# A transformer block on one Trainium2 core: four attention pieces moved by one or two steps among the matmuls of the feed-forward part

## The chip, the cores and the metric

The kernel runs on one core of a Trainium2 chip. The core has five engines with instruction queues of their own: TensorE (PE in the profile; its weight loads are PEld), VectorE (DVE), ScalarE (ACT), GpSimd (POOL) and SyncE (SP). Each engine works through its queue in order and waits for the others only by semaphores. The metric is device time in microseconds for one execution, and lower is better.

## What is computed

Eight batches of attention over 576 positions with 8 heads of 64 columns; heads 0 to 3 look at the last 32 positions (the "plain" heads), heads 4 to 7 at every fourth of the last 128 positions (the "dilated" heads). The result, as 4608 rows of 512, goes through two matrices of 512 x 2048 and 2048 x 512 with x·sigmoid(x) between them. Inputs and output are float32.

```python
def _attn_ref(q, k, v):                      # (8, 8, 576, 64)
    scores = scale * np.matmul(q, k.transpose(0, 1, 3, 2))
    rel = pos[:, None] - pos[None, :]
    mask_plain = (rel >= 0) & (rel < window)                                  # window 32
    mask_dil = (rel >= 0) & (rel < window * dilation) & (rel % dilation == 0) # dilation 4
    masks = np.stack([mask_plain if h < H // 2 else mask_dil for h in range(H)], axis=0)
    scores = np.where(masks[None, :, :, :], scores, -1000000000.0)
    scores = scores - np.max(scores, axis=-1, keepdims=True)
    attn = np.exp(scores)
    attn = attn / (np.sum(attn, axis=-1, keepdims=True) + 1e-09)
    return np.matmul(attn, v).astype(np.float32)

def _moe_ref(x, w_in, w_out):                # x: (4608, 512)
    h = x @ w_in
    g = h * (1.0 / (1.0 + np.exp(-h)))
    return (g @ w_out).astype(np.float32)
```

## The kernel before

The kernel goes through the batches 0 to 7. For each it runs layer 1 of the feed-forward part (`layer1`, 16 slices `f` of 128 hidden columns, each of 8 matmuls and one Silu on ScalarE into `gT`) and layer 2 (`layer2`, one row tile `t` of 128 rows after the other, 16 matmuls each, then `store`: a copy from PSUM to `ob` on VectorE and a DMA out on SyncE's queue). Batch 0 is cut in two halves in layer 1 (`layer1_part`), and its layer 2 (`layer2_first`) goes round its first four tiles in groups of four matmuls, in the order of tiles 0, 2, 1, 3. Odd batches take five tiles (4 to 8), since two batches share nine tiles of rows; even batches take four.

The attention of later batches is written in between, by hand. Every batch `b` has a table, `plan_of(b)`, that says at which step which function is issued: `at(step, function, arguments)`. `plan(s)` issues what the table holds for step `s`, in the order in which `at` was called. A step of layer 1 is one slice `f` (steps 0 to 15, 8 matmuls of 128x288); a step of layer 2 is four matmuls of 128x512 (steps 16 on, four to a row tile). In batch 0 the steps from -16 to 15 are the two halves of layer 1, and 16 to 31 the groups of layer 2. What a step issues comes ahead of that step's own matmuls. No planner reorders anything: the order of the calls is the order in each engine's queue (`tc.manual_schedule()`); semaphores only add the waits for data and for buffers.

For a batch `b` and a half `z` of the heads (`z` 0 plain, `z` 1 dilated) the functions are, in their order:

- `load_qk`, `load_v`, `shift_v`: DMAs on POOL's queue (batch 1's `shift_v` on SP's) into `n` (queries and keys as they lie in memory) and `vw` (values).
- `transpose(b, z, which, copies)`: 36 or so TensorE transposes of `n` (L274) for keys and as many for queries, and two copies each from PSUM to `kT`/`qT` (L278) or `kC`/`qC` (L287), by the engines in `copies`.
- `scores(b, z)`: 72 or 80 small matmuls (L324 plain, L336 dilated) into PSUM `s` and `ss`; then on VectorE scale and mask into `ms` (L448, L457) and the negated maxima `nm` (L464).
- `shift(b, z, hi)` (batch 1's dilated half alone) and `exps(b, z, hi)`: the exponentials on ScalarE, with their sums `l`; one instruction for each of 8 or 10 slots (L496), or one in all where `shift` went before (L487).
- `normal(b, z, hi)`: on VectorE the reciprocal `r` of the sums (L509, L510; with L505 a sum ahead of it where `shift` was used) and the weights `pn` (L512).
- `turn(b, z, hi)`: 4 or 5 TensorE transposes of `pn` (L521); `turned`: a copy of them from PSUM into `ptT` (L529).
- `values(b, z)`: 64 small matmuls (L554) and 8 or 16 more (L618) into PSUM `x` and `xs`; `finish`: casts of these into `xT` (L631, L623, L625), which layer 1 of that batch reads.

PSUM has two pools: `big` (two buffers of two banks) for the two layers' results, and `ps` (four buffers of one bank) for everything of the attention. The buffers of a pool are handed out in turn, in the order of the calls.

`plan_of(0)` holds the rest of batch 0's attention and all of batch 1's; `plan_of(1)` all of batch 2's, and of batch 3 the plain transposes, scores and exponentials; `plan_of(2)` to `plan_of(6)` the rest of batch `b + 1` and the beginning of batch `b + 2`. `later` writes the steps of `normal`, `turn`, `turned`, `values` and `finish`: its four numbers are the steps of the two `normal`, of both turns, and of the values. Without other `copies`, `later` gives the `turned` copies and the casts to VectorE.

Of the kernel before, what the change touches and what calls it, by code (L numbers as in the profile page):

```python
# [28 lines left out]
def kernel(  # L29
# [690 lines left out]
    dve, act = both = (nc.vector.tensor_copy, nc.scalar.copy)  # L720

    def transposes(at, b, z, step):
        for which in (1, 0):
            at(step, transpose, b, z, which, both)

    def later(at, b, z, steps, copies=(nc.vector.tensor_copy, nc.vector.tensor_copy)):

        for hi in (0, 1):
            at(steps[hi], normal, b, z, hi)
        for hi in (0, 1):  # L730
            at(steps[2], turn, b, z, hi)
        for hi in (0, 1):
            at(steps[2], turned, b, z, hi, copies[hi])
        at(steps[3], values, b, z)
        at(steps[3], finish, b, z, copies)

    def plan_of(b):
        ev = {}

        def at(s, fn, *args):  # L740
            ev.setdefault(s, []).append((fn, args))

        def all_exps(b, z):
            for hi in (0, 1):
                at(16, exps, b, z, hi)

        if b == 0:

            at(-16, normal, 0, 1, 1)
            at(-15, shift_class, 0, dve, 1, 2)  # L750
            at(-14, normal, 0, 0, 1)
            at(-13, clear_v, 1, nc.vector)
            at(-13, load_v, 1)
            for c in (2, 3):
                at(-13, load_w_out, c)
            at(-13, load_qk, 2)
            at(-8, turn, 0, 1, 1)
            at(-8, turned, 0, 1, 1, act)
            at(-6, values0, 1, 1)
            at(-6, last_values, 0, 1, (1,))  # L760
            at(-6, finish0, 1, 1)
            at(-6, last_finish, 0, 1, 1)
            at(-4, turn, 0, 0, 1)
            at(-4, turned, 0, 0, 1)
            at(-2, values0, 0, 1)
            at(-2, last_values, 0, 0, (1,))
            at(-2, finish0, 0, 1, both)
            at(-2, last_finish, 0, 0, 1)
            transposes(at, 1, 1, 2)
            at(8, scores, 1, 1)  # L770
            for hi in (0, 1):
                at(8, shift, 1, 1, hi)
            for which in (1, 0):
                at(16, transpose, 1, 0, which, (dve, dve))
            at(19, scores, 1, 0)
            at(14, shift_v, 1, nc.sync.dma_start)
            at(15, load_qk, 3)
            at(15, load_v, 2)
            at(15, shift_v, 2, nc.gpsimd.dma_start)
            all_exps(1, 1)  # L780
            for hi in (0, 1):
                at(19, exps, 1, 0, hi)
            for n, z, hi in ((20, 1, 0), (20, 1, 1), (26, 0, 0), (28, 0, 1)):
                at(n, normal, 1, z, hi)
            for n, z, copies in ((27, 1, (dve, dve)), (30, 0, both)):
                for hi in (0, 1):
                    at(n, turn, 1, z, hi)
                for hi in (0, 1):
                    at(n, turned, 1, z, hi, both[hi])
                at(n + 1, values, 1, z)  # L790
                at(n + 1, finish, 1, z, copies)
        elif b == 1:
            transposes(at, 2, 0, 2)
            transposes(at, 2, 1, 10)
            transposes(at, 3, 0, 15)
            at(7, scores, 2, 0)
            at(17, load_qk, 4)
            at(17, load_v, 3)
            at(17, shift_v, 3, nc.gpsimd.dma_start)
            at(13, scores, 2, 1)  # L800
            all_exps(2, 0)
            all_exps(2, 1)
            at(23, scores, 3, 0)
            at(23, exps, 3, 0, 0)
            at(23, exps, 3, 0, 1)
            later(at, 2, 0, (22, 24, 27, 28))
            later(at, 2, 1, (29, 31, 33, 34))
        else:
            if b + 2 < B:
                at(16, load_v, b + 2)  # L810
                at(16, shift_v, b + 2, nc.gpsimd.dma_start)
            if b + 1 < B:
                if b == 2:
                    for n in (0, 1):
                        at(1 + 2 * n, transpose, 3, 1, 1 - n, both)
                later(at, b + 1, 0, (0, 0, 4, 6))
                if b + 3 < B:
                    at(16, load_qk, b + 3)
            if b + 2 < B:
                transposes(at, b + 2, 0, 14)  # L820
                at(17, scores, b + 2, 0)
                at(18, exps, b + 2, 0, 0)
                at(18, exps, b + 2, 0, 1)
            if b + 1 < B:
                at(11, scores, b + 1, 1)
                all_exps(b + 1, 1)
                later(at, b + 1, 1, (22, 24, 27, 28))
            if b + 2 < B:
                transposes(at, b + 2, 1, 30)

        def plan(s):
            for fn, args in ev.pop(s, ()):
                fn(*args)

        return plan
# [58 lines left out]
    for b in range(B):  # L894
        plan = plan_of(b)
        if b == 0:
            for x in range(NFF):
                plan(2 * x - NFF)
                plan(2 * x + 1 - NFF)
                layer1_part(2 * x % NFF, 2 * x // NFF, None if x else warm)  # L900
        else:
            for f in range(NFF):
                plan(f)
                layer1(b, f)
        if b == 0:
            layer2_first(plan)
        else:
            layer2(b, plan)
        for s in range(NFF, 3 * NFF):
            plan(s)  # L910
# [30 lines left out]
```

## Time and profile before

| | us |
|---|---|
| median of three runs | 325.57 (325.37 to 326.73) |
| the profiled execution | 326.71 |
| its span, first to last instruction | 324.9 |
| TensorE busy in it (matmuls) | 309.6 |
| ScalarE, VectorE, POOL busy | 214.9, 179.8, 83.3 |

The stages of the span and how busy the engines were in each, from the windows of the trace:

| us from the start | what runs on TensorE | PE busy | DVE busy | ACT busy | DMA share |
|---|---|---|---|---|---|
| 12 to 41 | batch 0's attention and layer 1 | 26.9 of 29.0 | 21.0 | 20.3 | 1.34 |
| 41 to 61 | layer 2 of batch 0, batch 1's attention | 18.9 of 20.0 | 17.3 | 11.7 | 1.20 |
| 61 to 103.4 | batch 1's layers, attention of 2 and 3 | 41.3 of 42.4 | 25.9 | 36.1 | 0.69 |
| 103.4 to 141 | batch 2's layers, attention of 3 and 4 | 36.9 of 37.6 | 22.6 | 28.7 | 0.62 |
| 254.6 to 288 | batch 6's layers, attention of 7 | 33.1 of 33.4 | 15.4 | 19.7 | 0.09 |
| 288 to 325 | batch 7's layers | 33.2 of 37.0 | 4.2 | 10.7 | 0.12 |

The DMA share is the mean number of packets in work on each of the 16 DMA engines; over 1 means that packets overlap. A group of matmuls ends, by the trace's model, some 0.1 to 0.2 us after the next group has begun, so starts are compared with starts. The span and the profiled execution's time differ by what lies before the first and behind the last instruction (1.8 us).

### The profile page before, as it was taken

To read this page: it belongs to the slowest core of one execution; us is meant where nothing else is said; L and a number is where in the kernel's file an instruction comes from. 1 tells how busy PE (TensorE), PEld (TensorE's weight loads), DVE (VectorE), ACT (ScalarE), POOL (GpSimd) and SP (SyncE) were. 2 spreads that over 40 slices of the span, in tenths; PEclk is the share of its full clock that TensorE was granted. 3 is DMA by queue.
4 is the path that set the end of the run, shared out by engine and by line. 5 is a ranking of instruction groups with operands and counts; after the bars stand their busy time and mean duration, and the time that the engine had idled before them with its cause. 6 is when DMAs were issued, how large, how long until landed. Compare 5 with 4: busy or idle time off the path is not lost.

```text
span 324.9 us, 11768 instructions
## 1 busy us (share of the span) xinstructions
PE 309.6 (95%) x5151; PEld 200.5 (62%) x5151; DVE 179.8 (55%) x379; ACT 214.9 (66%) x700; POOL 83.3 (26%) x140
## 2 busy tenths in 40 slices
PE   5679989999989999999999999999999999999995
PEld 2458745677446774577645776567745776467544
DVE  6896679736497555762675446672577423530011
ACT  2676657666998568975797458985699357726300
POOL 8536537418304430245005600051000000000000
PEclk9679999999999999999999999999999999999999
DMA  8999999928924990298219850191011100110021
GB/s 110 184 214 204 190 230 202 234 70 130 173 86 77 134 146 2 100 148 133 45 65 121 182 88 2 67 170 39 5 39 62 65 4 0 68 67 0 2 97 67
DMA packets 45668, 32.63 MB, mean 100 GB/s; under 512 B 21264, under 2 KB 40336, under 8 KB 45616
## 3 DMA queue, kind: packets, MB, share of 16 engines
q0 software_dynamic: 39520, 21.73, 48.7%
q1 hardware_dynamic: 5952, 10.08, 8.4%
q8 instruction: 40, 0.66, 0.8%
q14 instruction: 12, 0.10, 0.1%
q10 hardware_dynamic: 144, 0.07, 0.1%
HBM read 37.75 MB, written 9.44 MB: 145 GB/s over the span
## 4 chain that ended last, share of the span: by engine, by line
PE 83%; DVE 6%; ACT 5%; DMA 3%; issue 2%; POOL 1%; POOLq 0%
PE h L644 35%; PE o L707 30%; PE h L664 4%; PE t L274 3%; ACT pe L496 3%; PE x L554 3%; DMA n<-in_q_dram 2%; PE pt L521 2%; DVE pn L512 1%; PE s L324 1%; PE o L681 1%; PE s L336 1%; DVE ms L448 1%; DVE nm L464 1%; PE x L580 1%
## 5 line engine op out<-in xcount | busy, mean ns | idle before, releaser
L644 PE MATMUL h<-xT,w_in 128*128 128x288 f16 x896 | 115.6, 286 | 0.7 <-issue 0.7
L707 PE MATMUL o<-w_out,gT 128*128 128x512 f16 (+1 forms) x528 | 115.6, 373 | 0.0
L652 ACT ACTIVATE gT<-h 128x576 f16<-128x576 f32 x112 | 73.0, 651 | 63.7 <-PE h L644 63.0
L644 PEld LDWEIGHTS <-w_in 128*128 128x128 f16 x896 | 85.6, 98 | 23.9 <-issue 1.0
L496 ACT ACTIVATE pe<-ms,nm 128x64 f32<-128x64 f32 x246 | 81.6, 333 | 3.3 <-DVE nm L464 3.2
L707 PEld LDWEIGHTS <-gT 128*128 128x128 f16 x528 | 50.1, 98 | 53.0
L691 DVE COPY ob<-o 128x512 f32<-128x512 f32 (+1 forms) x36 | 24.5, 682 | 53.4 <-PE o L707 53.1
L496 ACT ACTIVATION_READ_ACCUMULATOR pe<-ms,nm 128x1 f32 x246 | 45.9, 187 | 0.0
L448 DVE SCALAR_TENSOR_TENSOR ms<-s,mask 128x512 f32<-128x512 f32 x28 | 19.2, 686 | 44.2 <-PE s L336 26.1
L127 POOL DMA_DIRECT2D vw<-in_v_dram x16 | 10.1, 639 | 79.2 <-PE x L554 78.0
L512 DVE TENSOR_TENSOR pn<-pe,r 128x640 f16<-128x640 f32 (+2 forms) x32 | 25.3, 792 | 1.1
L631 DVE CAST xT<-x 128x512 f16<-128x512 f32 x27 | 17.4, 685 | 11.2 <-PE xs L618 11.2
L464 DVE TENSOR_REDUCE nm<-ms 128x10 f32<-128x640 f32 (+1 forms) x28 | 22.0, 787 | 1.0
L106 POOL DMA_DIRECT2D n<-in_k_dram x28 | 16.6, 607 | 15.5 <-PE t L274 5.9
L106 POOL DMA_DIRECT2D n<-in_q_dram x28 | 16.4, 606 | 10.1 <-DMA w_out<-in_moe_w_out_dram 5.3
L664 PE MATMUL h<-xT,w_in 128*128 128x256 f16 (+1 forms) x128 | 17.1, 286 | 1.3 <-ACT gT L671 1.3
L529 DVE COPY ptT<-pt 128x640 f16<-128x640 f16 (+1 forms) x27 | 11.8, 468 | 8.2 <-PE pt L521 8.0
L664 PEld LDWEIGHTS <-w_in 128*128 128x128 f16 x128 | 12.1, 98 | 5.1 <-issue 2.0
L681 PE MATMUL o<-w_out,gT 128*128 128x512 f16 x64 | 14.8, 380 | 0.1
L671 ACT ACTIVATE gT<-h 128x512 f16<-128x512 f32 (+1 forms) x16 | 10.3, 650 | 6.9 <-PE h L664 6.8
L521 PE MATMUL pt<-ident,pn 128*128 128x128 f16 x152 | 12.4, 224 | 1.4 <-DVE pn L512 1.4
L274 PEld LDWEIGHTS <-n 64*64 64x64 f16 (+1 forms) x840 | 10.0, 101 | 5.5 <-issue 5.1
(102 smaller groups left out, 264.7 us busy)
## 6 DMA issues: line engine op xcount, KB each, us to landing
out_dram<-ob SPq DMA_DIRECT2D x35, 256.0 KB, 2.0
n<-in_k_dram POOLq DMA_DIRECT2D x28, 144.0 KB, 5.5
n<-in_q_dram POOLq DMA_DIRECT2D x28, 144.0 KB, 5.7
vw<-in_v_dram POOLq DMA_DIRECT2D x8, 288.0 KB, 6.5
vw<-in_v_dram POOLq DMA_DIRECT2D x16, 128.0 KB, 4.2
w_in<-in_moe_w_in_dram POOLq DMA_DIRECT2D x4, 512.0 KB, 12.1
w_out<-in_moe_w_out_dram POOLq DMA_DIRECT2D x4, 512.0 KB, 10.6
vw<-vw POOLq DMA_DIRECT2D x12, 128.0 KB, 3.4
```

Source lines behind the costliest of these rows:

```text
L106: nc.gpsimd.dma_start(out=qk[b, z, which][i * HF : i * HF + UPS[z]].rearrange("p h u d -> p h (u d)"), in_=src[b, h : h + 2].rearrange("h ...
L274: nc.tensor.transpose(dst, w, ident[r, r])
L448: nc.vector.scalar_tensor_tensor(out=ms[:, 0:8].rearrange("p (n t) c -> p n (t c)", n=2), in0=s[hi].rearrange("p n t c -> p n (t c)"), sca ...
L464: nc.vector.tensor_reduce(out=nm[:, 0:w], in_=ms[:, 0:w], axis=AX.X, op=ALU.max, negate=True)
L496: nc.scalar.activation(pe[:, t, :], slot(t), AF.Exp, scale=1.0 if b else scale, bias=nm[:, t : t + 1], accum_out=l[:, t : t + 1],)
L512: nc.vector.tensor_tensor(pn[:, 0:w], a["pe", z, hi][:, 0:w], r[:, 0:w, None].broadcast_to([P, w, KB]), ALU.mult)
L521: nc.tensor.transpose(t[:, i, :], a["pn", z, hi][:, 2 * i : 2 * i + 2].rearrange("p t c -> p (t c)"), ident)
L644: nc.tensor.matmul(h[:, half, 0:HS], w_in16[:, c, f * P : f * P + P], xT[:, c, half * HS : half * HS + HS], start=(c == 0), stop=(c == MC ...
L652: nc.scalar.activation(gT[:, f, s0 : s0 + S].rearrange("p (a c) -> p a c", a=2), h[:, :, 0:HS], AF.Silu)
L664: nc.tensor.matmul(h[:, i, 0 : c1 - c0], w_in16[:, c, (f + i) * P : (f + i + 1) * P], xT[:, c, c0:c1], start=(c == 0), stop=(c == MC - 1),)
L691: copy(ob, o)
L707: nc.tensor.matmul(o, gT[:, f, t * P : (t + 1) * P], w_out16[:, f, m0:m1], start=(f == 0), stop=(f == NFF - 1),)
```

## The change

Four pieces of the table get other steps. No function changes, and no instruction is added or taken away.

- Batch 1 (table of batch 0): the plain transposes go from step 16 to 17, the plain scores and exponentials from 19 to 20. The dilated half's values and casts go from 28 to 29 (`n + 1 + z` with `z` 1); the plain half's stay at 31.
- Batch 3 (table of batch 1): plain scores and exponentials from step 23 to 21, ahead of the first `normal` of batch 2's plain half (22).
- Batch 3 (table of batch 2): dilated scores from step 11 to 10.
- Batch 7 (table of batch 6): turn and `turned` of the dilated half from step 27 to 28, values and casts from 28 to 29.

```diff
@@ plan_of, b == 0
             for which in (1, 0):
-                at(16, transpose, 1, 0, which, (dve, dve))
-            at(19, scores, 1, 0)
+                at(17, transpose, 1, 0, which, (dve, dve))
+            at(20, scores, 1, 0)
...
             for hi in (0, 1):
-                at(19, exps, 1, 0, hi)
+                at(20, exps, 1, 0, hi)
...
-                at(n + 1, values, 1, z)
-                at(n + 1, finish, 1, z, copies)
+                at(n + 1 + z, values, 1, z)
+                at(n + 1 + z, finish, 1, z, copies)
@@ plan_of, b == 1
-            at(23, scores, 3, 0)
-            at(23, exps, 3, 0, 0)
-            at(23, exps, 3, 0, 1)
+            at(21, scores, 3, 0)
+            at(21, exps, 3, 0, 0)
+            at(21, exps, 3, 0, 1)
@@ plan_of, b >= 2
-                at(11, scores, b + 1, 1)
+                at(10 if b == 2 else 11, scores, b + 1, 1)
                 all_exps(b + 1, 1)
-                later(at, b + 1, 1, (22, 24, 27, 28))
+                later(at, b + 1, 1, (22, 24, 28, 29) if b == 6 else (22, 24, 27, 28))
```

## The prediction, made before the changed kernel was run

> **What bounds the kernel now.** I read the page first (here its span, its busy times and its instruction queue), then the waits of TensorE alone (who waited for whom, us in total, times, longest), then the timeline around each wait (start, duration, engine, line, operation, in brackets the idle time before it), and last the packet times of the instruction queue.
>
> ```profile
> span 324.9 us, 11768 instructions
> PE 309.6 (95%) x5151; PEld 200.5 (62%) x5151; DVE 179.8 (55%) x379; ACT 214.9 (66%) x700; POOL 83.3 (26%) x140
> ...
> q8 instruction: 40, 0.66, 0.8%
> ```
>
> ```profile
> PE pt L521 <- DVE pn L512: 1.4, 2, 1.1
> PE h L664 <- ACT gT L671: 1.3, 1, 1.3
> PE t L274 <- issue: 0.8, 1, 0.8
> PE h L644 <- issue: 0.7, 1, 0.7
> ```
>
> TensorE is busy 95% of the span, and after the first 40 us it stops at only four places that are worth naming: twice for `pn` (1.11 and 0.33 us), and twice for "issue", which is no engine and no DMA (0.83 us at L274, 0.70 us at L644). A step that moves work is worth what it does to one of these four, or to a wait that it makes.
>
> What is "issue"? 0.66 MB in 40 packets is 16.4 KB each, and 10,302 TensorE instructions over 40 packets are 258 each, so queue 8 brings TensorE's program in blocks of about 256 instructions, 128 pairs of load and matmul. Counted in the trace, the two pauses come at weight loads 739 and 2276, which are 12 x 128 + 1 apart: both are block edges. The block for the first was fetched from 40.26 to 41.15 us and TensorE went on at 42.61; the block for the second from 121.13 to 122.06, and it went on at 123.38. So a block is usable 1.3 to 1.5 us after it landed. In both cases the fetch began late: 4.0 and 4.2 us after the preceding edge, with DMA loads running. With the DMA engines idle it began about 1.0 to 1.4 us after TensorE was 16 pairs short of the edge.
>
> **Part A, batch 1** (plain transposes 16 to 17, plain scores and exps 19 to 20, dilated values and finish 28 to 29). TensorE's timeline there:
>
> ```profile
> 41.23 0.54 PE L274 MATMUL t<-ident,n 64*64 64x64 f16 x44
> 42.61 0.41 PE L274 MATMUL t<-ident,n 64*64 64x64 f16 x28 [0.83 <-issue]
> 42.95 2.76 PE L681 MATMUL o<-w_out,gT 128*128 128x512 f16 x12
> 45.65 0.68 PE L324 MATMUL s<-kT,qT 64*32 64x64 f16 x64
> ...
> 53.26 0.88 PE L521 MATMUL pt<-ident,pn 128*128 128x128 f16 x10
> ```
>
> The pause falls 44 transposes into the 72. One step is four 128x512 matmuls; the 28 ahead of part B's scores (81.22 to 87.35) took 6.13 us, 0.87 a step. After the change these four run ahead of the transposes, so the same edge comes 40 transposes in, at about 41.23 + 0.9 + 0.3 = 42.45. The block is usable at 42.61 as before: the pause shrinks from 0.83 to about 0.1. But the transposes then end at 43.0, as before, twelve matmuls still stand between them and the scores, and the scores start at 45.7 as before. From there VectorE works without a hole from 46.40 to 59.25 (scores, sums, `pn`, `ptT`, casts of `xT`, stores, in its own timeline), and layer 1 of batch 1 starts at 60.88 behind its last casts. That chain starts no sooner, so TensorE only reaches the turn of the dilated part 0.87 earlier, at 52.4, and waits for `pn` (ready 53.62) instead. The values at 29 let `ob` of tile 0 go before the casts on VectorE; the same 3.07 us of work lies between 56.2 and 59.25, in another order. The copies of the transposed `kT`,`qT` (1.42 + 1.41 us) end at 45.5, 0.2 before the scores. The exps follow the scores on ScalarE, and the two `pn` of the dilated part still stand behind the scores' VectorE work. Taken: **0.0**. Bounds: -0.83 (the whole pause kept as gain) to +0.87 (pause not a fetch: it travels, and the chain starts a step later). I take the middle, since both ends need the fetch or the full VectorE to be misread.
>
> **Part B, batch 3's plain scores from 23 to 21 in batch 1's steps.**
>
> ```profile
> 87.35 0.68 PE L324 MATMUL s<-kT,qT 64*32 64x64 f16 x64
> 87.85 0.27 PE L324 MATMUL ss<-kT,qT 64*32 64x64 f16 x8
> 88.05 3.63 PE L707 MATMUL o<-w_out,gT 128*128 128x512 f16 x16
> 91.51 0.39 PE L521 MATMUL pt<-ident,pn 128*128 128x128 f16 x4
> 93.01 0.45 PE L521 MATMUL pt<-ident,pn 128*128 128x128 f16 x5 [1.11 <-DVE pn L512]
> ```
>
> The turn waits for a `pn` that VectorE reaches late, behind 3.06 us of score work (88.11 to 91.17) and an `ob` copy. Two steps earlier the scores start at 85.62 and VectorE at 86.38, 1.73 sooner; but `pn` of the first half (86.17 to 87.30, 1.13 us, until now done before the scores) then stands behind them. In sum: 86.38 + 3.06 + 1.10 + 0.63 (`ob`, overlapped) + 1.19 = 92.3 against 92.95. The wait goes from 1.1 to about 0.5: **-0.6**. The first half's `pn` is ready at 90.5, one microsecond before its turn at 91.51. Inputs of the scores are there since 81.6. ScalarE runs exps without a hole from 83.38 to 101.9 either way. Bounds: -1.1 (wait gone) to 0.
>
> **Part C, batch 3's dilated scores from 11 to 10 in batch 2's steps.** Nothing waits there for scores. But the block edge ahead of load 2276's lies in them (load 2147, at 116.94). With eight 128x288 matmuls fewer ahead of it (0.98 us, less eight more score pairs), this edge comes 0.85 us earlier, and the next fetch can begin at 120.3 instead of 121.13 (the same 4.2 us behind its edge) and be usable at 120.3 + 0.9 + 1.3 = 122.5, while TensorE reaches load 2276 at 122.3 to 122.6. **-0.7.** Bounds: -0.8 to 0.
>
> **Part D, batch 7's turn 27 to 28, values 28 to 29.**
>
> ```profile
> 281.76 0.44 PE L521 MATMUL pt<-ident,pn 128*128 128x128 f16 x5
> 282.53 0.45 PE L521 MATMUL pt<-ident,pn 128*128 128x128 f16 x5 [0.33 <-DVE pn L512]
> 282.82 1.03 PE L707 MATMUL o<-w_out,gT 128*128 128x512 f16 x4
> 283.78 0.71 PE L554 MATMUL x<-ptT,vw 64*64 64x32 f16 x64
> ```
>
> A step later the turn starts at 282.63 and finds `pn` ready (282.47). From its first matmul to the next group's it took 1.06 instead of the 0.56 of batch 2's turn at 99.26: 0.50 is saved. But `ob` of tile 2 now goes ahead of the two `ptT` copies on VectorE (0.69 from about 282.8, then 0.89), which end at 284.4; TensorE is there at 283.19 + 0.96 = 284.15 and waits 0.25, with the last tile's twelve matmuls and all of layer 1 queued behind the values. **-0.25.** Bounds: -0.5 to +0.1. The casts to `xT` end at 286.6, layer 1 of batch 7 starts after 287.
>
> No moved step issues a DMA. POOL's loads that reuse batch 1's `n` start at 49.28, six microseconds after the transposes that read it, and its loads after the values start at 77.75 at the soonest.
>
> **Sum:** 0.0 - 0.6 - 0.7 - 0.25 = -1.55, so the span goes from 324.9 to about 323.4. The profiled execution took 326.71, the median 325.57; the difference is taken from the median: **324.0**. About 0.5% (1.63 us) is what a measurement of this kernel can tell from no change; the limits are 323.9 and 327.2.
>
> **Rivals.**
>
> R1, the pauses aren't fetches. Then the first travels with the transposes (+0.83, VectorE's chain a step later) and the second stays: 0.83 - 0.6 - 0.25 = 0.0, **325.6**. For it: the profile names no cause. Against: both pauses stand 128-pair multiples apart, in the middle of a tile, where no buffer and no load can hold TensorE. [...]
>
> R2, the second fetch starts no sooner, because it waits for the loads to drain: at 121.0 they did drain. For it: the same at 190.27. Against: at 83.78 and 46.34 a fetch began amid loads. C gives 0: **324.7**.
>
> R3, batch 1's VectorE chain has slack that I don't see, and A's 0.83 stays gained: **323.2**. For: TensorE's own waits there are 0.1 to 0.3. Against: no hole on VectorE.
>
> R4, slower. In part A the request for the block after load 739 goes out 0.9 us later, behind more loads. It is needed at load 867, which TensorE now reaches at 49.0, with 0.9 of slack before `pn`. Fetch 1.2 and 1.3 until usable: a start by 47.4 costs nothing (it was 46.34), each microsecond later costs one, and from 48.95 on the kernel is slower. Behind the key load issued at 41.52, which landed at 52.04, it would start at 51: +3.6, **327.6**. Against: the fetch of before went past key loads that landed at 51.32.
>
> **Chances.** Forecast 0.55 (its own range 323.5 to 324.5), R1 0.14, R2 0.15, R3 0.10, R4 0.06. The range 323.0 to 325.6 takes in R1 to R3 and leaves out R4 and the ends of the others. Faster by over 0.5%: 0.30 of the forecast, all of R3, 0.02 of R2, 0.42. Slower: R4 and 0.02 of R1, 0.08. The rest, 0.50, is within.
>
> **What would show it.** A: fewer than 0.2 us of "issue" in L274 near 42.5, scores at 45.7, and a wait of about 0.9 at the dilated turn. B: the wait before the second five transposes about 0.5. C: no "issue" before L644 in batch 2, its block landing before 121.5. D: no wait at batch 7's turn, about 0.25 at its values. Scores of batch 1 at 46.5 would make A's reading wrong; a pause that stays in batch 2, C's.

## The result, and the profile after

The changed kernel took 325.06 us (median of 20 runs, 323.34 to 326.57), the kernel before 326.1 in the 20 runs beside it (325.25 to 328.37): a ratio of 0.9967, with a 95% interval of 0.9953 to 0.9982, which is 0.6 to 1.5 us less. A second comparison, told below, gave 0.9948 (0.9928 to 0.9968). Both intervals leave out 1, so it is faster, but by less than the 0.5% that I had named as the limit of what can be told in the first comparison and by about that much in the second.

The page of the changed kernel, its span and busy times:

```profile
span 322.8 us, 11769 instructions
PE 311.8 (97%) x5151; PEld 202.0 (63%) x5151; DVE 180.1 (56%) x379; ACT 214.7 (67%) x700; POOL 83.2 (26%) x140
```

Its waits of TensorE (who waited for whom, us in total, times, longest), the two rows that can be set beside those of before:

```profile
PE pt L521 <- DVE pn L512: 1.2, 2, 0.7
...
PE h L664 <- ACT gT L671: 0.5, 1, 0.5
```

Both rows with "issue" are gone. There are still two waits for `pn`, but other ones: the 0.7 is new and stands in batch 1, the other 0.44 is what is left of the 1.11. The wait at L664 lies in batch 0, where nothing was moved; it was 1.3 before and is 1.2 in a second trace of the changed kernel, so its 0.8 is no effect of the change. TensorE's timeline of the changed kernel at the four places (start, duration, engine, line, operation, idle time before it):

```profile
41.88 0.93 PE L274 MATMUL t<-ident,n 64*64 64x64 f16 x72
...
45.44 0.68 PE L324 MATMUL s<-kT,qT 64*32 64x64 f16 x64
...
52.30 0.44 PE L521 MATMUL pt<-ident,pn 128*128 128x128 f16 x5
53.48 0.45 PE L521 MATMUL pt<-ident,pn 128*128 128x128 f16 x5 [0.74 <-DVE pn L512]
...
85.40 0.68 PE L324 MATMUL s<-kT,qT 64*32 64x64 f16 x64
...
92.11 0.45 PE L521 MATMUL pt<-ident,pn 128*128 128x128 f16 x5 [0.44 <-DVE pn L512]
...
120.14 2.13 PE L644 MATMUL h<-xT,w_in 128*128 128x288 f16 x16
122.11 1.03 PE L707 MATMUL o<-w_out,gT 128*128 128x512 f16 x4
...
280.73 0.72 PE L521 MATMUL pt<-ident,pn 128*128 128x128 f16 x10
281.29 1.03 PE L707 MATMUL o<-w_out,gT 128*128 128x512 f16 x4
282.24 0.92 PE L554 MATMUL x<-ptT,vw 64*64 64x32 f16 x64
```

All 72 transposes of batch 1 now run in one piece, the plain scores start when they did before, and TensorE waits at the dilated turn instead. Batch 3's plain scores start 4.41 us behind layer 2 of batch 1 (80.99 to 85.40) instead of 6.13. The last 16 matmuls of batch 2's layer 1 have no hole. Batch 7's turn runs in one piece, and its values take 0.92 where they take 0.71 elsewhere.

Spans of single executions differ by a microsecond or more (324.0 to 326.0 in eleven runs of the kernel before), so the parts are read from stages: from the first matmul of one thing to the first of another, which a late start of the kernel does not touch. The stages are A, from batch 1's dilated scores to its layer 1; B, from layer 2 of batch 1 to layer 1 of batch 2; C, from layer 1 to layer 2 of batch 2; D, from layer 2 of batch 6 to layer 1 of batch 7. Stage 4, from layer 1 to layer 2 of batch 4, is the same code in all kernels of the table. The rows that begin and end B and C, first of the kernel before, then of the changed one:

```profile
81.22 6.21 PE L707 MATMUL o<-w_out,gT 128*128 128x512 f16 x28
...
103.30 1.14 PE L644 MATMUL h<-xT,w_in 128*128 128x288 f16 x8
...
123.88 1.03 PE L707 MATMUL o<-w_out,gT 128*128 128x512 f16 x4
```

```profile
80.99 4.48 PE L707 MATMUL o<-w_out,gT 128*128 128x512 f16 x20
...
102.41 1.14 PE L644 MATMUL h<-xT,w_in 128*128 128x288 f16 x8
```

C of the changed kernel ends at 122.11, shown above. The table is worked out from unrounded starts, so it can differ from these rows by 0.01.

| us | A | B | C | stage 4 | D |
|---|---|---|---|---|---|
| before | 24.85 | 22.09 | 20.58 | 18.81 | 15.74 |
| after | 24.92 | 21.41 | 19.71 | 18.69 | 15.45 |
| after, second trace | 24.91 | 21.41 | 19.71 | 19.29 | 15.45 |
| A alone | 24.76 | 22.09 | 20.42 | 19.09 | 15.74 |
| B alone | 24.61 | 21.41 | 20.09 | 19.07 | 15.74 |
| C alone | 25.12 | 22.09 | 19.74 | 19.09 | 15.74 |
| D alone | 24.60 | 22.09 | 20.80 | 18.87 | 15.45 |
| B, C and D | 24.66 | 21.41 | 19.70 | 18.68 | 15.45 |

### The profile page after: what moved, and what is told of

Same layout as the page of the kernel before. It is cut to its first block, busy times and chain, and to the rows that moved or that the text cites. A ratio compares the mean times of both kernels' runs of the same rounds, so it can differ in the third digit from the quotient of the medians.

```text
span 322.8 us, 11769 instructions
## 1 busy us (share of the span) xinstructions
PE 311.8 (97%) x5151; PEld 202.0 (63%) x5151; DVE 180.1 (56%) x379; ACT 214.7 (67%) x700; POOL 83.2 (26%) x140
## 4 chain that ended last, share of the span: by engine, by line
PE 87%; DVE 6%; ACT 3%; issue 1%; POOL 1%; DMA 1%; POOLq 0%
PE h L644 35%; PE o L707 33%; PE h L664 4%; PE t L274 3%; PE x L554 3%; PE pt L521 2%; PE o L681 2%; PE s L336 2%; PE s L324 1%; DVE pn L512 1%; DVE ms L448 1%; ACT pe L496 1%; DVE nm L464 1%; PE x L580 1%; DVE ob L691 1%
## 5 line engine op out<-in xcount | busy, mean ns | idle before, releaser
L691 DVE COPY ob<-o 128x512 f32<-128x512 f32 (+1 forms) x36 | 24.6, 682 | 52.5 <-PE o L707 52.1
L106 POOL DMA_DIRECT2D n<-in_q_dram x28 | 16.4, 605 | 10.0 <-DMA w_out<-in_moe_w_out_dram 5.4
L664 PE MATMUL h<-xT,w_in 128*128 128x256 f16 (+1 forms) x128 | 17.9, 295 | 0.5 <-ACT gT L671 0.5
L664 PEld LDWEIGHTS <-w_in 128*128 128x128 f16 x128 | 12.5, 101 | 4.7 <-issue 1.2
L521 PEld LDWEIGHTS <-pn 128*128 128x128 f16 x152 | 10.1, 99 | 4.7 <-DVE pn L512 1.5
```

The lines of the kernel that those rows point to most:

```text
L106: nc.gpsimd.dma_start(out=qk[b, z, which][i * HF : i * HF + UPS[z]].rearrange("p h u d -> p h (u d)"), in_=src[b, h : h + 2].rearrange("h ...
L521: nc.tensor.transpose(t[:, i, :], a["pn", z, hi][:, 2 * i : 2 * i + 2].rearrange("p t c -> p (t c)"), ident)
L664: nc.tensor.matmul(h[:, i, 0 : c1 - c0], w_in16[:, c, (f + i) * P : (f + i + 1) * P], xT[:, c, c0:c1], start=(c == 0), stop=(c == MC - 1),)
L691: copy(ob, o)
```

## The experiments

**Each part alone.** Four kernels, each with one of the four pieces of the diff shown above and nothing else.

```diff
# A alone                                     # B alone
+at(17, transpose, 1, 0, ...)                 +at(21, scores, 3, 0)
+at(20, scores, 1, 0); at(20, exps, ...)      +at(21, exps, 3, 0, 0); at(21, exps, 3, 0, 1)
+at(n + 1 + z, values, ...); (finish same)
# C alone                                     # D alone
+at(10 if b == 2 else 11, scores, b + 1, 1)   +later(at, b + 1, 1, (22, 24, 28, 29) if b == 6 else ...)
```

> Part A alone (batch 1: plain transposes, scores and exps a step later, dilated values a step later). Theory T (the pause in L274 is the fetch of an instruction block, and VectorE's chain bounds this stage): the 0.83 us of issue in the plain transposes goes to under 0.3, the plain scores still start 45.4 to 45.8 us from the start, TensorE waits about 0.9 at the dilated turn instead, layer 1 of batch 1 starts within 0.2 us of before; time 0.0 us against before, ratio 1.000 (0.999 to 1.001). Rival R1 (no fetch): the pause travels with the transposes, layer 1 of batch 1 starts 0.8 later, ratio 1.0025. Rival R3 (VectorE's chain has slack): 0.8 earlier, ratio 0.9975.

Measured: ratio 0.9999 (0.9981 to 1.0017). TensorE's timeline of A alone:

```profile
41.94 0.89 PE L274 MATMUL t<-ident,n 64*64 64x64 f16 x72
...
45.46 0.68 PE L324 MATMUL s<-kT,qT 64*32 64x64 f16 x64
...
53.42 0.45 PE L521 MATMUL pt<-ident,pn 128*128 128x128 f16 x5 [0.77 <-DVE pn L512]
```

The pause is gone and comes back as a wait of 0.77 at the dilated turn. Stage A takes 24.76 to 24.92 in the three traces with part A and 24.60 to 25.12 in the five without. Neither R1 (0.8 more) nor R3 (0.8 less) is in it.

> Part B alone (batch 3's plain scores at step 21 of batch 1 instead of 23). Theory T: the wait before the second five transposes of batch 2's plain turn goes from 1.1 to about 0.45 us, the stretch from layer 2 of batch 1 to layer 1 of batch 2 gets 0.65 shorter; ratio 0.998. The pause at the end of batch 2's layer 1 stays at about 0.7. Rival: if the whole wait is VectorE's score work, it goes to 0 and the stretch gets 1.1 shorter, ratio 0.9965; if the wait only moves to the values or casts, 0, ratio 1.000.

Measured: ratio 0.9987 (0.9962 to 1.0012). Stage B is 21.41 in all four traces that have part B and 22.09 in all four that don't: 0.68 less, with a wait of 0.43 left. That the pause in batch 2 would stay at 0.7 was a miss: here it was 0.2. This trace also has a pause of 0.65 that was not expected, at 79.90 among batch 3's transposes (L274), ahead of stage B and at a block edge that no part touches; the kernel before has 0.03 there. The wait and the pause in batch 2, in TensorE's timeline of B alone:

```profile
92.38 0.45 PE L521 MATMUL pt<-ident,pn 128*128 128x128 f16 x5 [0.43 <-DVE pn L512]
...
122.27 0.66 PE L644 MATMUL h<-xT,w_in 128*128 128x288 f16 x4 [0.21 <-issue]
```

> Part C alone (batch 3's dilated scores at step 10 of batch 2 instead of 11). Nothing waits for these scores. Theory T (instruction block requested sooner): the issue pause of about 0.7 to 0.9 us in batch 2's layer 1 is gone and its block lands at least 0.7 before it is needed; layer 2 of batch 2 starts 0.8 earlier than in before, counted from layer 1 of batch 2; ratio 0.9975. Rival R1 or R2: the pause stays, ratio 1.000.

Measured: ratio 0.9989 (0.9971 to 1.0007), no pause, stage C 19.74. Without part C the stage took 20.58, 20.42, 20.09 and 20.80, with it 19.70 to 19.74. So the pause is not a fixed price: by the stage it cost 0.35 to 1.1 us in these four traces (0.21 to 0.92 in the rows of "issue"), and in all four traces of the table that have part C it is gone. The packet times and the weight loads say why, for the block that load 2276 needs:

```
              edge before   fetch began, landed   TensorE went on
before        116.94        121.13   122.06       123.38
B alone       116.31        119.96   120.93       122.27
C alone       116.04        118.80   120.96       no pause
after         115.12        118.39   119.55       no pause
```

The times are from each trace's own start, so what counts is the distance to the edge before. From that edge to the next, TensorE takes 6.37 us with part C; without C it was through with the block's loads after 5.3 (116.94 to 122.28 in the kernel before) and stood. So C gives the fetch about 1 us more. In the two traces with C shown here the fetch also began 2.8 and 3.3 us behind the edge before, amid loads (DMA share 1.0 to 1.2 in the two us ahead of it), instead of 3.6 to 4.3 in the four without. The margin is thin: in C alone the block was crossed 1.59 us after it had landed. One later kernel with part C, the one without part A's transposes and scores told at the end, has the pause again. Its fetch began only 4.6 us behind the edge before, stage C took 20.21, and its waits have the row:

```profile
PE h L644 <- issue: 0.3, 1, 0.3
```

So C shrinks the pause by about 1 us and removed it in eight of nine traces; it doesn't rule it out.

> Part D alone (batch 7's dilated turn and values a step later). Theory T: no wait of TensorE at batch 7's turn, about 0.2 us at its values, where the copies of the turned weights now stand behind a store copy on VectorE; layer 1 of batch 7 starts 0.25 to 0.3 earlier, counted from layer 2 of batch 6; ratio 0.999, too small for this measurement. Rival: the wait for the copies eats all of it, 0.0.

Measured: ratio 0.9989 (0.9972 to 1.0006), which alone tells nothing; stage D is 15.45 in every trace with part D and 15.74 in every one without: 0.29 less. The turn has no wait, and the values stretch to 0.92, 0.2 more than elsewhere.

**The block edges moved.** The kernel before, with 24 small matmuls at its start (5.09 to 5.77 us).

```diff
-    keep_busy(big.tile([P, 2, 512], F32, tag="big", name="busy"), 4)
+    busy = big.tile([P, 2, 512], F32, tag="big", name="busy")
+    keep_busy(busy, 4)
+    for _ in range(24):
+        nc.tensor.matmul(busy[:, 0, 0:16], ident, ident[:, 0:16], start=True, stop=True)
```

> The kernel before with 24 small matmuls (16 columns) more at its very start, where TensorE waits for the first loads. They shift every block edge by 24 pairs and change nothing else. Theory T (pauses are fetches at block edges): the pause in batch 1's plain transposes comes after about 20 of the 72 instead of 44, and is again 0.8 to 1.1 us; the pause in batch 2 leaves layer 1's last slice and comes in the plain transposes of batch 4, after about 60 of the 72, and as TensorE gets there 2.2 us sooner while the fetch does not, it is 1 to 2.3 us. Rival R1 (the pause belongs to an instruction or a buffer): both stay where they were, after 44 transposes and four matmuls before the end of layer 1, at 0.8 and 0.7.

Measured: 332.33 us in the only run (the kernel before beside it: 325.08 to 328.28), a span of 330.6 instead of 324.9: with 24 matmuls of 0.7 us in all, the span is 5.6 longer. TensorE's timeline of it:

```profile
15.98 0.82 PE L314 MATMUL t<-ident,n 80*64 80x80 f16 x19 [1.42 <-issue]
...
22.18 0.29 PE L580 MATMUL x<-ptT,vw 64*64 64x32 f16 x6 [1.68 <-issue]
...
50.23 0.25 PE L324 MATMUL ss<-kT,qT 64*32 64x64 f16 x8 [1.92 <-issue]
...
123.54 0.68 PE L274 MATMUL t<-ident,n 64*64 64x64 f16 x60
126.41 0.29 PE L274 MATMUL t<-ident,n 64*64 64x64 f16 x12 [2.20 <-issue]
...
163.05 0.25 PE L274 MATMUL t<-ident,n 64*64 64x64 f16 x7 [0.91 <-issue]
```

The pause in batch 2 stands where the theory put it, after 60 of the 72 transposes and 2.20 long; layer 1's end has none. New pauses stand at other edges, multiples of 128 pairs apart, in four groups of small matmuls that did not pause in the kernel before; all five pauses ended 1.30 to 1.53 us after the end of a fetch (20.85 and 22.18, 125.11 and 126.41, for two). That settles the cause: the pause belongs to the place in the program's count, not to an instruction or a buffer. One half of the expectation missed: batch 1's transposes did not pause after 20, because the new pauses had made TensorE 3 us late by then, and the block (landed 42.42) lay ready.

**Is part A worth anything?** The changed kernel without A, the changed kernel again, and one with VectorE relieved, on one chip.

> The changed kernel without part A. Theory T: A is worth nothing because VectorE's chain bounds that stage, so this is as fast as the changed kernel: layer 1 of batch 1 starts within 0.2 us of the changed kernel's, counted from the dilated scores of batch 1; the pause in L274 is back at about 0.8, the wait at the dilated turn below 0.2; ratio 0.996. Rival R3: 0.8 us slower than the changed kernel, 0.9985. Rival R4 (A costs, by a later block): faster than the changed kernel, 0.995 or less.

> The changed kernel again, on the same chip as the two beside it. By the stages of the first traces: A 0, B -0.67, C -0.84, D -0.29, ratio 0.9945. By the first comparison: 0.9967 (0.9953 to 0.9982). If C's pause differs from run to run in the kernel before (0.2 to 0.9 in the traces so far), 0.995 to 0.997, and the changed kernel's batch 2 shows no pause in this trace either.

Measured: without A 0.9954 (0.9935 to 0.9973), with A 0.9948 (0.9928 to 0.9968). Stage A is 24.66 and 24.91, 0.25 apart where 0.2 was expected; the five traces without part A lie between 24.60 and 25.12, so that is no difference. A gains nothing in this kernel that these traces can show. The changed kernel's second trace has no pause in batch 2, but 0.6 more in stage 4, which no part touches: that stage took 18.68 to 19.29 in the traces of the table, and those of 19.07 and more have rows of 0.2 to 0.4 us of "issue" in its dilated scores.

The third kernel starts VectorE's chain sooner, moves part B's scores one step more, and shares batch 7's copies:

```diff
-for n, z, hi in ((20, 1, 0), (20, 1, 1), ...): at(n, normal, 1, z, hi)
+for n, z, hi in ((19, 1, 0), (20, 1, 1), ...): at(n, normal, 1, z, hi)
-at(21, scores, 3, 0)          # and its exps
+at(20, scores, 3, 0)          # and its exps
-later(at, b + 1, 1, (22, 24, 28, 29) if b == 6 else ...)
+later(at, b + 1, 1, (22, 24, 28, 29) if b == 6 else ..., both if b == 6 else (dve, dve))
```

> The changed kernel with three steps more: the first sum and weights of batch 1's dilated half at step 19, ahead of the plain scores on VectorE (it idles there for about 1 us); batch 3's plain scores at step 20 instead of 21; batch 7's dilated copies and casts shared by VectorE and ScalarE. Theory T (VectorE's chain bounds batch 1's stage and batch 2's plain turn): the chain starts 1 us earlier, the wait of 0.74 at batch 1's dilated turn goes below 0.2 and layer 1 of batch 1 starts 0.5 to 0.9 earlier than in the changed kernel; the wait of 0.44 at batch 2's plain turn is gone, 0.4 to 0.55; the pause inside batch 7's values is gone, 0.2. In all 1.1 to 1.6 us less than the changed kernel, ratio 0.9915 to 0.993. Rival: in batch 1 the stage is bound by ScalarE's exps, which start 0.8 later here: 0 there, ratio 0.9945.

Measured: 0.9952 (0.9932 to 0.9972), no better than the changed kernel. Its timeline of TensorE:

```profile
52.44 0.72 PE L521 MATMUL pt<-ident,pn 128*128 128x128 f16 x10
...
55.47 0.69 PE L554 MATMUL x<-ptT,vw 64*64 64x32 f16 x63 [0.43 <-ACT ptT L529]
...
85.20 0.27 PE L324 MATMUL ss<-kT,qT 64*32 64x64 f16 x8
85.99 6.22 PE L707 MATMUL o<-w_out,gT 128*128 128x512 f16 x28 [0.52 <-PE ss L324]
```

The wait at the dilated turn is gone, but ScalarE's exps now end later and with them its half of the copies, so the values wait: the rival was right, stage A 24.83. And with the scores at step 20 the wait at batch 2's turn is gone, but 0.52 appears behind the scores. The profile names the scores as its cause; but there is a block edge there (load 1636), its block landed at 84.54, and 85.99 is 1.45 later. Stage B is 21.39, the same as at step 21. Only batch 7 kept its 0.2 (stage D 15.24).

**The chain relieved where the waits now were.** From the changed kernel: the first weights at step 19 as above, both copies of the turned dilated weights to VectorE, which stood idle there for 1.07 us in the kernel just told, and the dilated casts to ScalarE. The second kernel has more: it takes the weights of batch 2's plain half at step 23 instead of 24, moves batch 5's dilated scores by one step, and shares batch 7's copies.

```diff
-for n, z, copies in ((27, 1, (dve, dve)), (30, 0, both)):
+for n, z, copies in ((27, 1, (act, act)), (30, 0, both)):
-    at(n, turned, 1, z, hi, both[hi])
+    at(n, turned, 1, z, hi, dve if z else both[hi])
...
# the second kernel alone, with batch 7's copies as above:
-later(at, 2, 0, (22, 24, 27, 28))
+later(at, 2, 0, (22, 23, 27, 28))
-at(10 if b == 2 else 11, scores, b + 1, 1)
+at({2: 10, 4: 12}.get(b, 11), scores, b + 1, 1)
```

> The changed kernel, with batch 1's stage relieved at the place that the run before showed (ScalarE's exps held the copy of the turned weights): first sum and weights of the dilated half at step 19, both copies of its turned weights on VectorE, all its casts to xT on ScalarE. Theory T: no wait of TensorE at the dilated turn, none over 0.2 at its values, and layer 1 of batch 1 starts 24.0 to 24.4 us behind batch 1's dilated scores instead of 24.9; the rest as in the changed kernel. Rival (the stage is bound by the exps of the plain half on ScalarE): 24.8 or more, the wait only moves to the plain turn. Ratio to the kernel before 0.992 to 0.994 by T, 0.995 by the rival.

> The same, with the weights of batch 2's second plain half at step 23 instead of 24 (ahead of a store copy on VectorE), batch 5's dilated scores at step 12 instead of 11 (so that the block edge among them comes a step later), and batch 7's copies and casts shared by VectorE and ScalarE. Theory T: no wait at batch 2's plain turn (0.44 in the changed kernel), no issue pause in batch 4's layer 1 (0.1 to 0.6 in the traces so far), no pause inside batch 7's values (0.2): 0.8 to 1.2 us less than the kernel beside it, ratio to the kernel before 0.988 to 0.991. Rival: these waits only move on to the next user, ratio as beside it.

Measured: 0.9926 (0.9906 to 0.9946) for the first, stage A 23.43; 0.989 (0.9866 to 0.9914), 322.72 us against 326.58, for the second, with stages 23.75, 20.94 (B), 18.93 (4) and 15.24 (D). TensorE's timeline of the first:

```profile
52.07 0.72 PE L521 MATMUL pt<-ident,pn 128*128 128x128 f16 x10
...
54.45 0.71 PE L554 MATMUL x<-ptT,vw 64*64 64x32 f16 x64
```

No turn and no values wait any more (0.3 is the most that any turn waits, at batch 2); the stage gave 1.5 us, more than expected. Three things were changed there at once, so the 1.5 is not divided among them. The second kernel is 1.5 us below the first by the medians, where 0.8 to 1.2 was expected. It beats the kernel before; with the changed kernel it was not run side by side, and its second comparison below (0.9892 to 0.9944) overlaps with that kernel's (0.9928 to 0.9968). In its stage 4 no row of issue is left, but the transposes behind the scores took 1.07 us instead of 0.83, so the edge was not wholly hidden there.

**Part A on top of that.** The second kernel with part A's transposes and scores back at 16 and 19, beside itself again. The dilated values stay at step 29, so of part A this takes back the transposes, scores and exponentials, and the first weights go a step earlier with them.

```diff
-at(17, transpose, 1, 0, which, (dve, dve)); at(20, scores, 1, 0); at(20, exps, 1, 0, hi)
+at(16, transpose, 1, 0, which, (dve, dve)); at(19, scores, 1, 0); at(19, exps, 1, 0, hi)
-for n, z, hi in ((19, 1, 0), ...
+for n, z, hi in ((18, 1, 0), ...
```

> The fastest kernel so far with batch 1's plain transposes, scores and exps back at steps 16 and 19 (and the first sum and weights at 18, so that VectorE's and ScalarE's order stay the same). Theory T: part A frees 0.8 us of TensorE, which the changed kernel loses again to VectorE's chain and which counts once that chain is relieved. So here the pause of 0.7 to 0.9 is back in L274, the scores start as early as with part A, and layer 1 of batch 1 starts 24.3 to 24.7 us behind the dilated scores instead of 23.4 to 23.8; ratio to the kernel before 0.991 to 0.992 instead of 0.989. Rival (part A is worth nothing in either case, as TensorE waits for VectorE or ScalarE anyway): 23.4 to 23.8, 0.989.

> The fastest kernel again, beside the one without part A, on the same chip: ratio to the kernel before 0.987 to 0.991, layer 1 of batch 1 23.4 to 23.8 us behind the dilated scores.

Measured: 0.993 (0.9905 to 0.9954) without A, 0.9918 (0.9892 to 0.9944) with it; stage A 24.08 without, and 23.43, 23.75 and 24.22 in the three traces with it. The pause in L274 was back (0.63), as expected. The sizes missed: the stage had been expected at 24.3 to 24.7 without A and, beside it, at 23.4 to 23.8 with A (here 24.22), and both ratios lie above those expected, with intervals that overlap. The third trace with A has another pause, at the next edge (load 867), in TensorE's timeline:

```profile
50.16 3.63 PE L681 MATMUL o<-w_out,gT 128*128 128x512 f16 x16 [0.22 <-issue]
```

Its block was fetched from 47.46 to 48.69 there, 4.05 us behind the preceding edge and 1.23 long, against 3.67 and 0.99 in the trace with 23.75. In all seven traces with part A this edge was crossed 1.38 to 1.53 us after its block had landed, in the six without it 1.71 to 2.38. So A takes away one pause and makes the next edge tighter; what it is worth once VectorE is relieved stays open, between -0.1 and 0.65 us.

## Why the prediction was right, point by point

**The bound and the four pauses.** "Issue" was the fetch of instruction blocks: the shifted edges show it (in batch 2 the pause came after 60 transposes and was 2.20 long), and R1 falls. The odd 1 between loads 739 and 2276 has a plain reason: two semaphore instructions stand between them in TensorE's queue (at 79.30 and 79.50 us in the trace of the kernel before). Counted in instructions, 1535 pairs and these two are 3072, and from the fetch at 40.26 up to the one at 121.13 queue 8 brought 12 packets: 256 instructions each. The fetch with idle DMA engines, put at 1.0 to 1.4 us after TensorE was 16 pairs short of the edge, does not hold throughout: in the kernel before seven fetches with the queues idle kept to it, three began 0.6 to 0.9 ahead of that point (204.88, 280.07, 305.62) and two 1.9 and 3.6 behind it (159.36, 124.49). No term of the sum used it.

**A, 0.0.** Right in size, and the steps forecast for it were seen: scores at 45.4 to 45.5, the pause turned into a wait of 0.74 (0.9 forecast), layer 1 of batch 1 within 0.1 of before. R3 falls: TensorE ran into VectorE's chain, and only kernels that started that chain sooner and relieved ScalarE got the stage below 24.6. The 0.0 was taken as the middle of -0.83 and +0.87, and identical code differs by 0.2 to 0.8 us in this stage, so the traces can't tell it from a tenth more or less. R4's mechanism is real but small. In the changed kernel the block after load 739 began at 46.34 as before, and the crossing of load 867 cost 0.3 more (0.53 between the two loads, 0.22 before; 0.81 in the second trace), inside the 0.9 of cover that I had named.

**B, -0.6.** Measured -0.68, with 0.44 of the wait left (0.5 forecast).

**C, -0.7.** On the mean over four traces without C the stage took 20.47, so -0.76. The mechanism is the one forecast, an earlier edge with more matmuls behind it. R2 falls: the fetch did start sooner, and amid loads. The delay behind the edge was off: 3.3 us in the changed kernel (2.8 in C alone) instead of the 4.2 taken over from the kernel before, and it ranged from 2.8 to 4.6 in the nine traces with part C. The prediction had one trace and one value of this term; that -0.7 came so close to a mean over pauses of 0.35 to 1.1 is in part luck.

**D, -0.25.** Measured -0.29, and the wait of 0.2 at the values is the one that I had put at 0.25.

**The sum, -1.55.** By the stages A +0.1, B -0.68, C -0.76, D -0.29: -1.6. By the clock -1.1 in the first comparison and -1.7 in the second (1 - 0.9948 of 326.4); the interval of the first (0.6 to 1.5) ends just short of the stages' sum, and the two intervals overlap. The pauses at edges that no part touched differ from execution to execution by 0.6 us in stage 4 alone. That this makes the two comparisons differ is likely, but was not tried by itself. The median of 325.06 lies 1.1 above the forecast of 324.0: the 20 runs put the kernel before at 326.1 instead of 325.57, and the rest is the smaller gain. It is inside the range of 323.0 to 325.6, but above the forecast's own 323.5 to 324.5 and nearer to R2's 324.7. So the time alone would not have told the forecast from R2 or R1; the stages and the fetches do.

## What to carry to other kernels

A pause that no engine and no DMA explains can be the program itself on its way, as the 0.83 and 0.70 us here: count the instructions ahead of it, and see whether pauses lie a fixed count apart (here 3072, 12 blocks). Then put long matmuls, not short ones, ahead of that edge, or let its predecessor be crossed sooner; with part C the way from edge to edge took 6.37 us instead of 5.3, and the pause, 0.70 before, was gone in eight of nine traces. Before moving work into a hole on the busiest engine, ask which other engine's chain starts behind it: as long as that chain ends the stage, the hole only moves (in part A 0.83 us of pause became a wait of 0.74).

## What was not expected of the hardware

TensorE's program came in blocks: in the kernel before, queue 8 brought 40 packets with 0.66 MB in all, 16.4 KB each, and 12 of them for the 3072 instructions from load 739 to load 2276, which is 256 to a block. A block was usable only some time after it had landed. In the 14 traces, from 12 us on, there are 27 pauses of 0.2 us and more at a block edge; TensorE went on 1.2 to 1.5 us after the landing in all of them, and it crossed no edge sooner than that. A fetch mostly took 0.9 to 1.4 us (2.5 at the most). With DMA loads running it began between the preceding edge and 4.6 us after it, in 25 of the 27 pauses 2.7 to 4.6 us after it; with the queues idle (a DMA share under 0.06 in the two us ahead of it) it began 1.6 us after that edge at the latest. That the running loads hold the fetch back is read from this; no run moved a load to try it. So 128 pairs of small matmuls, which TensorE got through in about 5.4 us, could outrun the fetch, by 0.2 to 2.2 us in these pauses. Where the edges fall is set by everything ahead of them: with 24 small matmuls more at the start, the one execution took 5.6 us more, and its last new pause stood at 163 us.
